# The opening of a linear-recurrence and feed-forward kernel: VectorE's queue in the order of the source, and half of the first stacking issued by ScalarE

## The chip, the core and the metric

The kernel runs on one core of a Trainium2 chip. The core has TensorE (PE: matrix products into PSUM; PEld is its loading of weights), VectorE (DVE), ScalarE (ACT), GpSimd (POOL) and SyncE (SP), each with its own queue of instructions that it runs in order, and 16 DMA engines that SP and ACT hand transfers to. The metric is device time in microseconds (us), the median of several runs; one more execution was recorded by the profiler, and the lines in this document are from it.

## The reference

For 4 batches, 8 heads, 768 tokens and head size 48, with a complex decay `a` per token and channel that is scaled to a magnitude of at most 0.999:

```python
mag = np.sqrt(a_re * a_re + a_im * a_im)
scale = np.minimum(mag, 0.999) / (mag + 1e-06)
a_re_n, a_im_n = (a_re * scale, a_im * scale)
for t in range(S):
    new_re = ar * S_re - ai * S_im
    new_im = ar * S_im + ai * S_re
    kv = np.einsum('bhd,bhe->bhde', k[:, :, t], v[:, :, t])
    S_re, S_im = (new_re + kv, new_im)
    y[:, :, t] = np.einsum('bhd,bhde->bhe', q[:, :, t], S_re)
```

Then `x`, the 3072 x 384 matrix of the `y`, goes through `(x @ w_a) * (x @ w_b) @ w_out` with `w_a`, `w_b` of 384 x 1536 and `w_out` of 1536 x 384. All in float32.

## The kernel before

The work is cut into 12 units: 2 pairs of batches times 6 chunks of 128 tokens. For each unit

- `scale(u)` works out the factor that limits the decay (ScalarE: squares, logarithms, exponentials; VectorE: the steps between, L178 to L192). In unit 0 it runs on two halves.
- `prep(u)` multiplies the decays up along the chunk (VectorE: `pr` and `z` at L226 and L232, the block products `pb` and `b_t` at L261 and L267, L288 and L293), takes magnitude and inverse (ScalarE L296, L303, L304 between VectorE's L293, L302, L317 and L319) and multiplies `q` and `k` by the result (`qk`, L308 and L323).
- `stack(u)` copies `qk` by ten small DMAs (eight heads, two of them in two pieces) into `stk`, with real and imaginary part of a head one below the other.
- `attn(u)` is the chunk's attention: scores on TensorE (L378), times a causal mask on VectorE (`am`, L381), outputs (L418), `x` split into a high and a low part (`xh`, `xl`; L422, L430, L433), and the carried state.
- The feed-forward: for each of 12 blocks `f` of 128 columns `gemm1` (L485, 18 products), the product of both halves on ScalarE and VectorE (`h_t`, `hh`, `hl`; L493 to L496), and two blocks later `gemm2` (L503, 6 products).

The weights come as float64 bits and are converted on the core, once, while unit 0 runs: `split_weights()` makes float32 from the bits with three VectorE instructions (L133, L135, L137, into one of three buffers `o_sb`), ScalarE rounds it to the high part (L141), TensorE forms the remainder (L146, L147), and ScalarE writes that as the low part (L148). There are 36 such conversions, three for each of the 12 blocks; `w26` is the third part of block 6. The first 21 (blocks 0 to 6) use `gemm1`'s three PSUM buffers `ab`, the others the buffers `pm` of the attention.

The order of the instructions on each engine is not the source's. A scheduler with its own model of costs puts every ready instruction in by priority (earlier in the source is more urgent, and `tc.high_priority` moves masks, `h_t` and casts further up). The order that comes out is fixed at build time. The source gives, ahead of the loop over the units: `scale(0)`, `prep(0)`, `stack(0)`, the conversions of blocks 0 to 5, then `attn(0)` with steps of `prep(1)`; in the loop of the first unit a block's conversions and a part of `prep(1)` stand ahead of each `gemm1`. `prep(u)` also runs `scale(u + 1)`. A unit's attention is interleaved with the feed-forward of the unit before.

Of the kernel before, what the change touches and what calls it, by code (L numbers as in the profile page):

```python
# [8 lines left out]
F32 = mybir.dt.float32  # L9
# [57 lines left out]
def tile_kernel(ctx: ExitStack, tc: tile.TileContext, a_d, qk_d, v_d, w_d, qn_d, kn_d, vn_d, an_d, out_d):  # L67
# [59 lines left out]
    def split_weights():  # L127
        for f in range(NF):
            for m, (c0, n) in enumerate(WPART):
                raw = raws[f, m]  # L130
                t = moe.tile([128, n], F32, name="o_sb", bufs=O_BUFS)
                tu = t.bitcast(U32)
                vec.tensor_scalar(out=tu, in0=raw[:, :, 1], scalar1=3, scalar2=0x3FFFFFFF,  # L133
                                  op0=ALU.logical_shift_left, op1=ALU.bitwise_and)
                vec.scalar_tensor_tensor(out=tu, in0=raw[:, :, 0], scalar=29, in1=tu,  # L135
                                         op0=ALU.logical_shift_right, op1=ALU.bitwise_or)
                vec.scalar_tensor_tensor(out=tu, in0=raw[:, :, 1], scalar=0xC0000000, in1=tu,  # L137
                                         op0=ALU.bitwise_and, op1=ALU.bitwise_or)
# [7 lines left out]
                pe.matmul(out=lp[:, 0:n], lhsT=ident, rhs=t, start=True, stop=False)  # L146
                pe.matmul(out=lp[:, 0:n], lhsT=r(nident), rhs=r(hi), start=False, stop=True)  # L147
                act.copy(out=r(lo), in_=lp[:, 0:n])  # L148
            yield


    bnext = {}
# [10 lines left out]
    halves = (slice(0, W // 2), slice(W // 2, W))  # L163
    z_first = zpool.tile([128, 3, W], F32, name="z")

    def scale(u, a_t, tmp):

        sc = zpool.tile([128, W], F32, name="sc")
        for n, hs in enumerate(halves if u == 0 else (slice(0, W),)):
            n = n and NU
            t = tmp[:, 0:2, hs]
            m, x, s0 = t[:, 0], t[:, 1], sc[:, hs]
            act.activation(out=t, in_=a_t[:, :, hs], func=AF.Square, accum_out=sums[:, u + n:u + n + 1])
            vec.scalar_tensor_tensor(out=m, in0=m, scalar=-EPS * EPS, in1=x, op0=ALU.add, op1=ALU.add)  # L178
            act.activation(out=s0, in_=m, func=AF.Ln, bias=b_sq)
            act.activation(out=s0, in_=s0, func=AF.Exp, scale=0.5)  # L180
            act.activation(out=s0, in_=s0, func=AF.Ln, bias=b_eps)
            act.activation(out=s0, in_=s0, func=AF.Exp, scale=-1.0)
            act.activation(out=x, in_=s0, func=AF.Square)
            yield 900
            vec.tensor_tensor(out=m, in0=m, in1=x, op=ALU.mult)
            act.activation(out=x, in_=s0, func=AF.Identity, scale=-EPS, bias=b_one)
            yield 900
            vec.scalar_tensor_tensor(out=m, in0=m, scalar=-0.5, in1=x, op0=ALU.mult, op1=ALU.add)
            yield 900
            vec.scalar_tensor_tensor(out=s0, in0=m, scalar=0.5, in1=s0, op0=ALU.add, op1=ALU.mult)  # L190
            yield 900
            vec.scalar_tensor_tensor(out=s0, in0=s0, scalar=0.999, in1=x, op0=ALU.mult, op1=ALU.min)  # L192
            yield 900
        sc_tiles[u] = sc

    def rescaled(c):
        return c % 2 == 1 and c + 1 < NCH

    def prep(u):
# [94 lines left out]
                              in0=view(pz[:], 0, PAIRS), in1=view(pz[:], W, PAIRS), op=ALU.add)  # L294
            yield 870
        act.activation(out=a_t, in_=z[:, 0:2], func=AF.Square)  # L296
        if rescaled(c):
# [7 lines left out]
        qk4 = qk[:, :, :, 0:2 * TOK].rearrange("p j s (x t) -> p j s x t", x=2)  # L305

        def times_p(k, x0, x1):
            vec.tensor_tensor(  # L308
                out=qk4[:, :, k, x0:x1], in0=qk4[:, :, 1, x0:x1],
                in1=z[:, k].rearrange("p (j t) -> p j t", j=NJ).unsqueeze(2).broadcast_to([128, NJ, x1 - x0, TOK]),  # L310
                op=ALU.mult)
# [25 lines left out]
    def stack(u):  # L337
        n = RUN if rescaled(u % NCH) else 2 * TOK
        for h in range(H):
            r0 = h * D  # L340
            while r0 < (h + 1) * D:
                j, p = divmod(r0, 128)
                m = min((h + 1) * D - r0, 128 - p)
                d0 = 2 * (r0 - h * D)
                sync.dma_start(out=stk[d0:d0 + 2 * m, h, 0:n], in_=qk[p:p + m, j, :, 0:n])
                r0 += m


    v_tiles = {}

    def load_v(u):
        for i in range(2):
# [11 lines left out]
    def attn(u, xh, xl):  # L364
# [8 lines left out]
        def scores(i, hg):  # L373
            qs, ks = cols(i)
            sp = ps_m.tile([128, 4, 128], F32, name="pm")
            for h4 in range(4):
                h = hg * 4 + h4
                pe.matmul(out=sp[:, h4], lhsT=stk[:, h, ks], rhs=stk[:, h, qs], start=True, stop=True)  # L378
            am = kvp.tile([128, 512], F32, name="am", bufs=2).rearrange("p (h t) -> p h t", h=4)
            with tc.high_priority(offset=ATTN_FIRST):  # L380
                vec.tensor_tensor(out=am, in0=sp, in1=mask[:].unsqueeze(1).broadcast_to([128, 4, 128]),  # L381
                                  op=ALU.mult)
            ams[i, hg] = am

        def transposes(i, hg):
# [260 lines left out]
    for w in range(NU):  # L646
        last = w + 1 == NU
        x_nxt = None if last else new_x()
        at = None if last else attn(w + 1, *x_nxt)
        if not last:  # L650
            load_v(w + 1)
        os_ = [ps_o.tile([128, 512], F32, name=f"o{t}") for t in range(2)]
        slots = [0, 2 * (STACK_AT[min(w, 4)] + 1 - max(ATTN_AT[min(w, 4)], 0 if w else P1_AT + 1))]
        left = [pieces(w + 1)]

        def slot():
            if at is None or f < ATTN_AT[min(w, 4)] or (w == 0 and f <= P1_AT) or not slots[1]:
                return
            n = -(-left[0] // slots[1])
            slots[1] -= 1  # L660
            for _ in range(n):
                next(at, None)
                left[0] -= 1

        for f in range(NF):
            if w == 0:
                next(ws, None)
                drain(p1, P1_F)
                if f == P1_AT:
                    drain(p1)  # L670
# [88 lines left out]
```

## Time and profile before

| | before |
|---|---|
| median of 3 runs | 700.21 us (699.59 to 700.63) |
| the profiled execution | 700.52 us, span 698.8 us |
| TensorE busy | 654.6 us (94%) |
| VectorE busy | 550.4 us (79%) |
| ScalarE busy | 311.4 us (45%) |

In the profile's lines a group is given as line, engine, operation, output<-input, shapes; in a timeline the first number is the start in us from the begin of the span, the second the duration in us, and the bracket at the end tells how long the engine had been idle and who ended that. `x2` means two instructions in a row. PEclk is TensorE's granted clock, 1.00 for full. SPq is SP handing out a DMA. A matmul in float32 that is not in the fast format shows as two records.

### The profile page before, as it was taken

The page shows a single profiled execution, that of the slowest core. Times are in us where ns is not written, and L with a number is a line of the kernel's source. Part 1 is how long each engine was busy: PE and PEld are TensorE (multiplying, and loading weights), DVE is VectorE, ACT ScalarE, POOL GpSimd, SP SyncE. Part 2 cuts the span into 40 slices and gives each one's busy share as a digit, 9 for nine tenths or more (in the row PEclk, how much of TensorE's full clock was granted, in tenths as well). Part 3 has the DMA queues.
Part 4 walks back from the last instruction along what each step waited for, and adds up shares of the span by engine and source line. Part 5 has one row for each costly group of instructions (what it writes and reads, how often), then busy time and mean ns, then how long its engine had stood idle before and what let it go on. Part 6 is the DMA issues. An engine that isn't in the chain of part 4 may idle for free.

```text
span 698.8 us, 14287 instructions
## 1 busy us (share of the span) xinstructions
PE 654.6 (94%) x5842; PEld 610.4 (87%) x5842; DVE 550.4 (79%) x1259; ACT 311.4 (45%) x622; POOL 5.6 (1%) x11
## 2 busy tenths in 40 slices
PE   3547999999999999999999999999999999999996
PEld 1224788799899999999999999999999999999996
DVE  6998899998888989989899798999989863233221
ACT  6357656634535446255363564534542332231221
POOL 3000000000000000000000000000000000000000
PEclk9567999999999999999999999999999999999999
DMA  8963300611414205124151340511510500300000
GB/s 312 403 262 93 120 1 0 180 58 58 130 38 130 81 21 157 58 88 132 32 161 45 93 143 2 166 69 47 135 55 2 162 27 17 106 23 2 24 1 27
DMA packets 30231, 63.93 MB, mean 91 GB/s; under 512 B 3664, under 2 KB 7248, under 8 KB 30160
## 3 DMA queue, kind: packets, MB, share of 16 engines
q1 hardware_dynamic: 26704, 58.23, 26.6%
q10 hardware_dynamic: 3456, 4.72, 1.9%
q8 instruction: 48, 0.79, 0.4%
q14 instruction: 23, 0.19, 0.1%
HBM read 39.32 MB, written 4.72 MB: 63 GB/s over the span
## 4 chain that ended last, share of the span: by engine, by line
PE 64%; DVE 26%; DMA 4%; ACT 3%; issue 2%; SPq 1%; DVEq 0%; ACTq 0%
PE ab L485 31%; PE o L503 15%; PE xp L418 6%; PE pm L378 4%; PE pm L441 4%; DVE a_t L288 2%; DMA w<-in_dram 2%; DVE pr L226 2%; DVE qk L308 2%; DVE h_t L494 2%; PE pm L389 2%; DVE hl L496 2%; DMA stk<-qk 1%; DVE am L381 1%; DVE z L232 1%
## 5 line engine op out<-in xcount | busy, mean ns | idle before, releaser
L485 PE MATMUL ab<-xh,w 128*128 128x256 f32 x1728 | 338.7, 285 | 0.0
L485 PEld LDWEIGHTS ab<-xh,w 128*128 128x128 f32 x1728 | 276.6, 189 | 1.9 <-issue 1.4
L485 PE MATMUL ab<-xl,w 128*128 128x256 f32 x864 | 244.6, 283 | 0.0
L485 PEld LDWEIGHTS ab<-xl,w 128*128 128x128 f32 x864 | 162.9, 189 | 0.5 <-ACT xl L433 0.2
L503 PE MATMUL o<-w,hh 128*128 128x384 f32 x576 | 152.4, 345 | 0.0
L493 ACT COPY h_t<-ab 128x256 f32<-128x256 f32 x144 | 53.3, 370 | 184.5 <-PE ab L485 184.1
L494 DVE TENSOR_TENSOR h_t<-ab,h_t 128x256 f32<-128x256 f32 x144 | 60.6, 421 | 70.5 <-ACT h_t L493 69.8
L503 PEld LDWEIGHTS o<-w,hh 128*128 128x128 f32 x576 | 96.8, 188 | 3.7 <-issue 2.8
L503 PE MATMUL o<-w,hl 128*128 128x384 f32 x288 | 97.6, 340 | 0.0
L495 ACT CAST hh<-h_t 128x256 fp32r<-128x256 f32 x144 | 58.0, 403 | 72.6 <-DVE h_t L494 71.4
L496 DVE TENSOR_TENSOR hl<-h_t,hh 128x256 fp32r<-128x256 f32 x144 | 60.6, 421 | 15.6 <-ACT hh L495 15.5
L378 PE MATMUL pm<-stk 128*128 128x128 f32 x384 | 55.3, 282 | 2.6 <-DMA stk<-qk 1.8
L146 PE MATMUL ab<-o_sb,ident 128*128 128x384 f32 x42 | 29.3, 797 | 29.9 <-DVE o_sb L137 29.9
L378 PEld LDWEIGHTS pm<-stk 128*128 128x128 f32 x384 | 49.6, 193 | 7.6 <-issue 4.2
L503 PEld LDWEIGHTS o<-w,hl 128*128 128x128 f32 x288 | 54.0, 188 | 0.1
L226 DVE TENSOR_TENSOR pr<-z 128x384 f32<-128x384 f32 (+1 forms) x91 | 47.2, 525 | 4.3 <-ACT z L212 2.5
L288 DVE TENSOR_TENSOR a_t<-z,b_t 128x768 f32<-128x768 f32 x48 | 45.1, 953 | 0.0
L146 PEld LDWEIGHTS ab<-o_sb,ident 128*128 128x128 f32 x42 | 10.2, 288 | 39.5 <-DVE o_sb L137 29.2
L418 PE MATMUL xp<-am,v_t 128*32 128x128 f32 x768 | 42.5, 277 | 2.1 <-DVE am L381 1.8
L308 DVE TENSOR_TENSOR qk<-qk,z 128x1536 f32<-128x1536 f32 (+1 forms) x26 | 42.3, 1628 | 0.1
L381 DVE TENSOR_TENSOR am<-pm,mask 128x512 f32<-128x512 f32 x48 | 32.8, 686 | 6.7 <-PE pm L378 6.6
L441 PEld LDWEIGHTS pm<-v_t,kt 128*96 128x96 f32 x320 | 32.2, 164 | 1.8 <-issue 1.4
(106 smaller groups left out, 758.7 us busy)
## 6 DMA issues: line engine op xcount, KB each, us to landing
w<-in_dram SPq DMA_DIRECT2D x36, 384.0 KB, 8.1
qk<-in_dram SPq DMA_DIRECT2D x12, 768.0 KB, 4.8
stk<-qk SPq DMA_DIRECT2D x48, 192.0 KB, 3.4
a_t<-in_dram SPq DMA_DIRECT2D x11, 768.0 KB, 4.4
v_t<-in_dram SPq DMA_DIRECT2D x24, 256.0 KB, 2.7
stk<-qk SPq DMA_DIRECT2D x24, 192.8 KB, 3.4
out_dram<-o_sb ACTq DMA_DIRECT2D x24, 192.0 KB, 1.9
stk<-qk SPq DMA_DIRECT2D x16, 128.0 KB, 3.1
```

Of the source, the lines that this page charges most:

```text
L226: vec.tensor_tensor(out=pr[:, :, :, o:o + n], in0=view(zz, W + at_(i) + 2 * o, [[W, 2], [-W, 2], [2, n]]), in1=tok(slice(1, 3), i - 1, o, ...
L288: vec.tensor_tensor(out=pz[:, s].rearrange("p (j b e) -> p j b e", j=SUB // 2, e=2), in0=zb[:, 1 + s], in1=view(bb, (1 + k - s) * NB, [[0, ...
L308: vec.tensor_tensor(out=qk4[:, :, k, x0:x1], in0=qk4[:, :, 1, x0:x1], in1=z[:, k].rearrange("p (j t) -> p j t", j=NJ).unsqueeze(2).broadca ...
L378: pe.matmul(out=sp[:, h4], lhsT=stk[:, h, ks], rhs=stk[:, h, qs], start=True, stop=True)
L418: pe.matmul(out=xp[qd * 32:(qd + 1) * 32, ti], lhsT=l, rhs=rr, start=st, stop=sp_, tile_position=(0, qd * 32), skip_group_check=True)
L441: pe.matmul(out=kp[0:KS, h4 * D:(h4 + 1) * D], lhsT=kts[i, hg][:, h4, :], rhs=v_t[:, o:o + D], start=True, stop=True)
L485: pe.matmul(out=ab[:, m * TOK:(m + 1) * TOK], lhsT=r(w_ab(f, part, m * NJ + i)), rhs=r(xt[:, i, :]), start=n == 0, stop=n == 8)
L493: act.copy(out=h_t, in_=ab[:, 0:TOK])
L494: vec.tensor_tensor(out=h_t, in0=ab[:, TOK:2 * TOK], in1=h_t, op=ALU.mult)
L495: act.copy(out=r(hh), in_=h_t)
L496: vec.tensor_tensor(out=r(hl), in0=h_t, in1=hh, op=ALU.subtract)
L503: pe.matmul(out=os_[tt][:, 0:DM], lhsT=r(ht[:, ts]), rhs=r(w_t[f, 2][:, part, :]), start=(f == 0 and n == 0), stop=(f == NF - 1 and n == 2))
```

## The change

Four things are changed, all in the first 150 us:

- VectorE's instructions from `scale(0)` to unit 0's fourth mask are issued under `tc.manual_schedule`: on VectorE they keep the order in which the source writes them. The conversions among them are put in by hand, in thirds (`split_weights` now yields ahead of each VectorE step), by the numbers `OPEN`.
- The two halves of `scale(0)` are generators of their own, and the multiplication of `qk` by the first power (`times_p(0, 0, 1)`) moves up by a few lines.
- Everything that VectorE gets after that, the rest of the conversions and of `prep(1)`, stands behind the last of the four masks (`tc.issue_after`); its order is the scheduler's again.
- In `stack(0)` the DMAs of the odd heads are handed out by ScalarE instead of SP.

```diff
+OPEN = (5, 1, 1, 2, 9, 3)
...
+                yield
                 vec.tensor_scalar(out=tu, in0=raw[:, :, 1], scalar1=3, scalar2=0x3FFFFFFF,
...
-            for k in range(2):
-                times_p(k, 0, 1)
+            times_p(1, 0, 1)
...
-                sync.dma_start(out=stk[d0:d0 + 2 * m, h, 0:n], in_=qk[p:p + m, j, :, 0:n])
+                eng = act if u == 0 and h % 2 else sync
+                eng.dma_start(out=stk[d0:d0 + 2 * m, h, 0:n], in_=qk[p:p + m, j, :, 0:n])
...
-    drain(scale(0, a_tiles[0], z_first))
-    drain(prep(0))
-    stack(0)
-    load_qk(1)
-    p1 = prep(1)
-    for _ in range(CONV_FIRST):
-        next(ws)
-    x_cur = new_x()
-    for _ in attn(0, *x_cur):
-        drain(p1, P1_A)
+    convert(1)
+    x_cur = new_x()
+    with tc.manual_schedule(engines={mybir.EngineType.DVE}):
...
+        next(g0)
+        next(g1)
+        convert(OPEN[0])
+        drain(g0)
+        convert(OPEN[1])
+        drain(g1)
+        p0 = prep(0)
+        for cost in p0:
+            if cost == 950:
+                convert(OPEN[2])
+            if cost == 1000:
+                convert(OPEN[3])
+        stack(0)
+        load_qk(1)
+        p1 = prep(1)
+        next(p1)
+        convert(OPEN[4])
+        next(p1)
+        convert(OPEN[5])
+        at = attn(0, *x_cur)
...
+    opening = latest[0].ins if hasattr(latest[0], "ins") else latest[0]
+    with tc.issue_after(opening):
+        convert(9 * CONV_FIRST - steps[0])
+        for _ in at:
+            drain(p1, P1_A)
```

Lines move a little: L133, L135, L137 become L135, L138, L141; the casts L141 and L148 become L145 and L152; L146 and L147 become L150 and L151; L178 to L192 become L180 to L194; L226 and L232 become L228 and L234; L308 becomes L302; L381 becomes L387; L485 becomes L491.

On VectorE, around the last step of the 21st conversion (of `w26`). Before (`o_sb_771` is its buffer, `w07` and `w17` are block 7):

```order
L133 TENSOR_SCALAR o_sb_771<-w26_168 128x384
L137 SCALAR_TENSOR_TENSOR o_sb_761<-w16_166,o_sb_761 128x384
L135 SCALAR_TENSOR_TENSOR o_sb_771<-w26_168,o_sb_771 128x384
L133 TENSOR_SCALAR o_sb_812<-w07_170 128x384
L137 SCALAR_TENSOR_TENSOR o_sb_771<-w26_168,o_sb_771 128x384
L135 SCALAR_TENSOR_TENSOR o_sb_812<-w07_170,o_sb_812 128x384
L137 SCALAR_TENSOR_TENSOR o_sb_812<-w07_170,o_sb_812 128x384
L133 TENSOR_SCALAR o_sb_822<-w17_172 128x384
L135 SCALAR_TENSOR_TENSOR o_sb_822<-w17_172,o_sb_822 128x384
L381 TENSOR_TENSOR am_519<-pm_514,mask_96 128x512
```

Now (`z_581` and `pr` are `prep(1)`, `a_t_144` and `sc_615` unit 2's `scale`):

```order
L135 TENSOR_SCALAR o_sb_773<-w26_168 128x384
L187 TENSOR_TENSOR a_t_144<-a_t_144 128x768
L228 TENSOR_TENSOR pr_642<-z_581 128x384
L138 SCALAR_TENSOR_TENSOR o_sb_773<-w26_168,o_sb_773 128x384
L234 TENSOR_TENSOR z_581<-pr_642 128x2x96
L190 SCALAR_TENSOR_TENSOR a_t_144<-a_t_144 128x768
L228 TENSOR_TENSOR pr_648<-z_581 128x384
L192 SCALAR_TENSOR_TENSOR sc_615<-a_t_144,sc_615 128x768
L234 TENSOR_TENSOR z_581<-pr_648 128x2x96
L194 SCALAR_TENSOR_TENSOR sc_615<-sc_615,a_t_144 128x768
L239 TENSOR_SCALAR z_581<-z_581 128x96
L141 SCALAR_TENSOR_TENSOR o_sb_773<-w26_168,o_sb_773 128x384
```

Before, that step stood ahead of unit 0's first mask; now it stands behind all four masks, seven steps of `prep(1)` and unit 2's `scale`.

On TensorE, at the first product of unit 0's feed-forward. Before, unit 0's attention (`xp`, `pm`) was in front of it and the 21st conversion 20 rows earlier:

```order
L418 MATMUL xp_587<-am_571,v_t_136 32x128 x6
L389 MATMUL pm_635<-ident_91,stk_108 128x96
L441 MATMUL pm_691<-v_t_134,kt_629 96x48 x4
L430 MATMUL xp_587<-xh_512,nident_115 128x384
L485 MATMUL ab_786<-xh_512,w00_336 128x256
```

Now the conversions of blocks 5 and 6 are in front of it:

```order
L150 MATMUL ab_572<-o_sb_566,ident_91 128x384
L151 MATMUL ab_572<-w25_570,nident_115 128x384
L150 MATMUL ab_759<-o_sb_576,ident_91 128x384
L151 MATMUL ab_759<-w06_757,nident_115 128x384
L150 MATMUL ab_769<-o_sb_763,ident_91 128x384
L151 MATMUL ab_769<-w16_767,nident_115 128x384
L150 MATMUL ab_779<-o_sb_773,ident_91 128x384
L151 MATMUL ab_779<-w26_777,nident_115 128x384
L491 MATMUL ab_790<-xh_201,w00_223 128x256
```

So the product that followed the attention now follows the last conversion of block 6.

On ScalarE, where the stacking is handed out (`a_t_118` and `sc_369` are unit 1's `scale`, `w01`, `w11` conversions of block 1):

```order
L179 ACTIVATE a_t_118,chk_104<-a_t_144 128x1536
L350 DMA stk_108<-qk_110 96x1x512 x2
L350 DMA stk_108<-qk_110 32x1x512
L350 DMA stk_108<-qk_110 64x1x512
L350 DMA stk_108<-qk_110 96x1x512
L181 ACTIVATE sc_369<-a_t_118,biases_99 128x768
L145 CAST w01_378<-o_sb_350 128x384
L182 ACTIVATE sc_369<-sc_369 128x768
L152 CAST w01_378<-ab_380 128x384
L183 ACTIVATE sc_369<-sc_369,biases_99 128x768
```

And on SP, whose queue had all weight loads and then ten stacking DMAs (the names in brackets are completion semaphores waited for; the first two stacking DMAs of ScalarE signal DMAHW4 and DMAHW6):

```order
L125 DMA w011_194<-in_3_dram 128x768 [waits DMAHW4_49]
L125 DMA w111_196<-in_3_dram 128x768 [waits DMAHW5_49]
L125 DMA w211_198<-in_3_dram 128x768 [waits DMAHW6_49]
L350 DMA stk_108<-qk_110 96x1x512 [waits DMAHW7_49,DVE_49]
L350 DMA stk_108<-qk_110 64x1x512 [waits DMAHW0_49]
L350 DMA stk_108<-qk_110 32x1x512 [waits DMAHW1_49]
```

Five stacking DMAs have moved from SP's queue into ScalarE's, between two steps of unit 1's `scale`; two of SP's last weight loads now wait for the first two of them.

More of the change, by code (lines that the diff above doesn't have):

```diff
@@ L148, in split_weights @@
                 act.copy(out=r(lo), in_=lp[:, 0:n])
-            yield
     bnext = {}
@@ L164, in tile_kernel @@
     z_first = zpool.tile([128, 3, W], F32, name="z")
[L166 to L193, printed above, removed]
@@ L296, in prep, with times_p @@
         act.activation(out=a_t, in_=z[:, 0:2], func=AF.Square)
+        qk4 = qk[:, :, :, 0:2 * TOK].rearrange("p j s (x t) -> p j s x t", x=2)
+        def times_p(k, x0, x1):
+            vec.tensor_tensor(
+                out=qk4[:, :, k, x0:x1], in0=qk4[:, :, 1, x0:x1],
+                in1=z[:, k].rearrange("p (j t) -> p j t", j=NJ).unsqueeze(2).broadcast_to([128, NJ, x1 - x0, TOK]),
+                op=ALU.mult)
+        if u == 0:
+            times_p(0, 0, 1)
+            yield 950
         if rescaled(c):
@@ L622, in tile_kernel, with convert @@
     ws = split_weights()
-    drain(scale(0, a_tiles[0], z_first))
-    drain(prep(0))
-    stack(0)
-    load_qk(1)
-    p1 = prep(1)
-    for _ in range(CONV_FIRST):
-        next(ws)
-    x_cur = new_x()
-    for _ in attn(0, *x_cur):
-        drain(p1, P1_A)
+    steps = [-1]
+    def convert(n):
+        for _ in range(n):
+            next(ws, None)
+            steps[0] += 1
+    convert(1)
+    x_cur = new_x()
+    with tc.manual_schedule(engines={mybir.EngineType.DVE}):
+        sc_first = zpool.tile([128, W], F32, name="sc")
+        g0, g1 = (scale(0, a_tiles[0], z_first, sc_first, n * NU, hs) for n, hs in enumerate(halves))
+        next(g0)
[18 more added lines that the diff above has]
+        at = attn(0, *x_cur)
+        for n in range(2):
+            next(at)
+        for n in range(3):
+            next(p1)
+        for n in range(4):
+            next(at)
+    opening = latest[0].ins if hasattr(latest[0], "ins") else latest[0]
[3 more added lines that the diff above has]
+            drain(p1, P1_A)
     pend = []
@@ L666, in tile_kernel @@
             if w == 0:
-                next(ws, None)
-                drain(p1, P1_F)
+                with tc.issue_after(opening):
+                    convert(9)
+                    drain(p1, P1_F)
+                    if f == P1_AT:
+                        drain(p1)
                 if f == P1_AT:
-                    drain(p1)
                     stack(1)
```

35 lines of the change are left out of this document (27 added, 8 removed).

## The prediction

> **What bounds the kernel now.** I read the busy times by stretch first, then TensorE's waits, then the rows of each engine in the first 150 us. Line numbers are those of the kernel before; "conversion" is one third of a weight block (L133, L135, L137 on VectorE, two casts on ScalarE, L146 and L147 on TensorE).
>
> ```profile
> core 0: us, PE busy (x) PEld busy (x) DVE busy (x) ACT busy (x) POOL busy (x), PEclk, DMA share, GB/s
> 0.00:77.00 77.00, 43.06 (x176) 23.70 (x176) 66.95 (x170) 42.53 (x80) 5.59 (x11) 0.76 0.72 259
> 77.00:160.00 83.00, 80.74 (x661) 72.25 (x661) 77.31 (x190) 47.77 (x99) 0.00 (x0) 1.00 0.20 60
> 160.00:300.00 140.00, 138.62 (x1358) 132.69 (x1357) 124.37 (x276) 65.44 (x122) 0.00 (x0) 1.00 0.28 84
> ```
> ```profile
> PE ab L146 <- DVE o_sb L137: 29.9, 13, 9.7
> ```
>
> From 77 us on TensorE is busy nearly without a gap, and stays so; before 77 us it waits, 29.9 us of it for VectorE's conversions. So what the opening costs is decided by when TensorE gets onto its dense work, and later stages give nothing back. The rows of TensorE (the first four from the timeline, the others from the chain of waits):
>
> ```profile
> 77.30 0.40 PE L485 MATMUL ab<-xh,w 128*128 128x256 f32 x2
> ...
> 82.79 0.81 PE L146 MATMUL pm<-o_sb,ident 128*128 128x384 f32 x2
> 83.14 0.63 PE L147 MATMUL pm<-w,nident 128*128 128x384 f32 x1
> 83.61 0.81 PE L146 MATMUL pm<-o_sb,ident 128*128 128x384 f32 x2
> ```
> ```profile
> 111.05 2.13 PE ab L485 x18
> 113.19 1.05 PE o L503 x6
> ...
> 130.99 0.49 PE pm L378 x2
> ...
> 149.56 0.43 PE ab L485 x3
> ```
>
> The first product of unit 0 starts at 77.30, the first of unit 1 at 149.56. In between lie 12 times 2.13 us of L485 (25.6), 12 times 1.05 us of L503 (12.6), 15 conversions of 0.82 us (start to start, 82.79 to 83.61; 12.3) and the attention of unit 1. Up to 130.99 (53.7 us) TensorE did all L485, ten L503 groups, the 15 conversions and 2.6 us of unit 0's attention: 51.0 us of work, so it ran 95% dense. The last 18.6 us are unit 1's attention with 2.3 us of L503 among it.
>
> **Where the change puts TensorE's start.** In the new order TensorE's first product of unit 0 stands directly behind L151 of the 21st conversion (block 6, third part). Before, that conversion was over at 63.4 us and the attention (76 to 77 us) was the last thing waited for. Now VectorE does far more ahead of it, so it becomes the gate. VectorE's rows:
>
> ```profile
> 8.42 0.56 DVE L135 SCALAR_TENSOR_TENSOR o_sb<-w,o_sb 128x384 uint32<-128x384 uint32 x1
> 9.02 0.56 DVE L137 SCALAR_TENSOR_TENSOR o_sb<-w,o_sb 128x384 uint32<-128x384 uint32 x1
> ...
> 11.56 0.55 DVE L185 TENSOR_TENSOR z<-z 128x384 f32<-128x384 f32 x1
> 12.03 0.55 DVE L137 SCALAR_TENSOR_TENSOR o_sb<-w,o_sb 128x384 uint32<-128x384 uint32 x1
> 12.80 0.56 DVE L188 SCALAR_TENSOR_TENSOR z<-z 128x384 f32<-128x384 f32 x1 [0.22 <-ACT z L186]
> ...
> 57.75 0.96 DVE L308 TENSOR_TENSOR qk<-qk,z 128x768 f32<-128x768 f32 x1
> 58.62 0.96 DVE L178 SCALAR_TENSOR_TENSOR a_t<-a_t 128x768 f32<-128x768 f32 x1
> ...
> 62.86 0.55 DVE L137 SCALAR_TENSOR_TENSOR o_sb<-w,o_sb 128x384 uint32<-128x384 uint32 x1
> ...
> 67.58 0.95 DVE L185 TENSOR_TENSOR a_t<-a_t 128x768 f32<-128x768 f32 x1
> ...
> 134.46 0.69 DVE L381 TENSOR_TENSOR am<-pm,mask 128x512 f32<-128x512 f32 x1 [0.36 <-PE pm L378]
> ```
> ```profile
> L226 DVE TENSOR_TENSOR pr<-z 128x384 f32<-128x384 f32 x14 | 7.8, 560 | 2.6 <-ACT z L212 2.3
> L381 DVE TENSOR_TENSOR am<-pm,mask 128x512 f32<-128x512 f32 x8 | 5.5, 686 | 1.4 <-PE pm L378 1.4
> L232 DVE TENSOR_TENSOR z<-pr 128x192 f32<-128x192 f32 x14 | 5.0, 357 | 0.2
> L188 DVE SCALAR_TENSOR_TENSOR a_t<-a_t 128x768 f32<-128x768 f32 x3 | 2.9, 953 | 0.0
> ```
>
> Neighbours overlap: 11.56 to 12.03 is 0.47 us for an instruction of 0.55, 57.75 to 58.62 is 0.87 for one of 0.96. So an independent instruction costs its duration less 0.09. One that reads its neighbour's result does not overlap: 8.42 to 9.02 is 0.60 where 0.47 would be due. I take 0.115 us more for each such pair, about the mean of the five that stand clear of other waits.
>
> - Base: L137 of the 21st conversion started at 62.86.
> - Added in front of it in VectorE's queue (counted in the two orders): the four masks L381 (4 x 0.60 = 2.4), nine 768-wide steps of `scale` (9 x 0.87 = 7.8), two L210 (1.7), seven pairs of L226 and L232 (7 x 0.73 = 5.1), less a step of a conversion (-0.3) and a short one (+0.1): 16.9 us.
> - Neighbours that depend: 65 pairs instead of 13, because conversions no longer stand between the steps of `prep(0)`. 52 x 0.115 = 6.0 us.
> - New waits. In the opening two naked waits for ScalarE's L186: 11.56 to 12.80 is 1.24, of which one conversion step filled 0.47 before: 2 x 0.77 = 1.5. For ScalarE's three steps between L293 and L317, which four conversion steps covered: 0.7 by the same bounds (0 to 2). In unit 2's `scale`: 0.5 (0 to 3). Waits of before that go: -0.9.
>
> The largest wait is unit 1's `scale`, whose five ScalarE steps now have the five stacking DMAs and casts ahead of or among them:
>
> ```profile
> 59.61 0.94 ACT L179 ACTIVATE sc<-a_t,biases 128x768 f32<-128x768 f32 x1 [0.21 <-DVE a_t L178]
> ...
> 63.37 0.48 ACT L148 CAST w<-ab 128x384 fp32r<-128x384 f32 x1 [0.71 <-PE ab L147]
> ```
> ```profile
> 58.74 6.78 SPq L345 DMA_DIRECT2D stk<-qk  x10
> ```
>
> Before, L178 to L185 took 8.96 us (58.62 to 67.58), the chain on ScalarE and casts that wait for TensorE (63.37, 0.71 us). VectorE has 5.1 us of work between these two in the new order (three conversions' worth of steps and L178 itself), so it stands at least 3.9 us; with five DMA issues of 0.68 us (6.78 / 10) ahead of the chain, of which 1.0 us is hidden, up to 6.3. I take 5.2. It can't wait below zero; if the casts no longer hold ScalarE, five steps of about 0.9 us (59.61) end after 5.2 us and the wait is near 0.
>
> New waits: 5.2 + 1.5 + 0.7 + 0.5 - 0.9 = 7.0 us. L137 of the 21st conversion then starts at 62.86 + 16.9 + 6.0 + 7.0 = 92.8, and from there the rest of L137 (0.55), the cast (0.5, as at 63.37) and L147 (83.14 to 83.61, 0.45) take 1.5 us: **94.3 us instead of 77.30**.
>
> **Unit 0's attention itself comes earlier, and that buys nothing.** 14 2/3 conversions of 1.21 us leave the front of the last L308: -17.7, +5.1 for 44 more dependent pairs, +1.3 net waits: it ends at about 47.4 instead of 58.7. The stacking: SP's row of ten DMAs becomes five on each queue, at best 3.4 us less. The masks follow only behind the wait of 5.2, at about 60 instead of 67. xh and xl are ready near 70, and TensorE may not use them until 94.
>
> **The sum.** From its start TensorE has, up to unit 1's first product, 25.6 + 10 x 1.05 + 12.3 + unit 1's attention (18.6 - 2.3 = 16.3 with its waits). In the new order three L485 groups stand among that attention, so its holes get filled; dense it would be 12.6. 61.0 dense, 64.7 as before; at 95% dense 64.2. Two L503 groups are left for later (2.1). 94.3 + 64.2 + 2.1 - 149.6 = +11.0 us. The profiled execution took 700.5 us (span 698.8), 0.3 above the median: **711**. After that both queues hold the same work, TensorE has no gaps to absorb a delay, and 0.2% (1.4 us) is what a measurement can tell from no change.
>
> [...]
>
> **Rivals.**
> 1. *VectorE's total, not TensorE's gate, sets the end (faster).* In the stretch before 135 us VectorE is the engine that TensorE meets. Its queue up to unit 1's first mask (134.46), added up as above, is 125.8 us, so 8.7 us are waits; the new queue to that mask is only 2.1 us longer (three h_t and hl pairs and some of `prep(2)` less, 46 more dependent pairs). If the new order has 5 us of waits, the end moves by 2.1 - 3.7 = -1.6: 698.9. It decides from 6.6 us of waits on downward. For it: VectorE is 87% busy before 77 us. Against: the 61 us that TensorE still has to do behind the gate.
> 2. *SP's half of the stacking arrives late (slower still).* In SP's new queue the last weight loads wait for ScalarE's stacking DMAs (they share completion semaphores), and SP's five stacking DMAs stand behind these loads. I have them landing some 11 us after the last L308, under the masks' 12.6. With loads as slow as the opening's (8.1 us to landing, below) they land at 16 us: +3.4, 714.5.
> [...]
> 4. *Hidden:* the gate opens at 77 as before, since the 17 us of added work were somehow run in idle time: 700.5. VectorE had about 10 us idle before 77, half of it ahead of the first data, so this needs a queue that isn't in order.
>
> ```profile
> w<-in_dram SPq DMA_DIRECT2D x36, 384.0 KB, 8.1
> ```
>
> **Chances and range.** My sum 66%, rival 1 10%, rival 2 12%, rival 3 8%, rival 4 4%. Slower by over 0.2%: 86% (the sum, 2, 3); within 0.2%: 6% (4 and the edge of 1); faster: 8% (1). The sum's own bounds: no new wait and dense TensorE gives 87.3 + 61.0 + 2.1 - 149.6 = +0.8; waits of 10 us and 67 us behind the gate give +17. Cutting the unlikely ends and keeping rivals 2 and 3: 703 to 718.
>
> **What would show it.** In the profile after: the last L308 of unit 0 (now L302) ends near 48; L187 of unit 1 about 10 us after L180, with VectorE idle some 5 us for ScalarE; the masks near 60; TensorE's first L491 at 94 (right if 90 to 98), with little on TensorE between 72 and 94; unit 1's first L491 near 159; from there the rows of before, some 11 us later. The forecast is wrong if that first L491 stands before 85, or if VectorE shows under 3 us of waits up to there.

## The result, and the profile after

The changed kernel takes 716.52 us (median of 4 runs, 716.39 to 716.87) where the kernel before takes 699.9 (4 runs, 698.8 to 700.63): 1.024 times as long, 95% interval 1.0222 to 1.0257. The forecast was 711 with a range of 703 to 718. The profiled execution spans 714.7 us against 698.8, so the traces compared here show 15.9 us of the difference. Line numbers below are those of the changed kernel: a conversion's three VectorE steps are L135, L138 and L141, TensorE's are L150 and L151, a mask is L387, a first-layer product L491.

First the busy times by stretch, in the columns of the prediction's first view:

```profile
core 0: us, PE busy (x) PEld busy (x) DVE busy (x) ACT busy (x) POOL busy (x), PEclk, DMA share, GB/s
0.00:77.00 77.00, 28.24 (x161) 17.18 (x162) 57.14 (x137) 32.45 (x60) 5.60 (x11) 0.96 0.74 263
77.00:160.00 83.00, 73.07 (x534) 58.79 (x532) 79.00 (x187) 51.47 (x105) 0.00 (x0) 0.92 0.17 48
160.00:300.00 140.00, 139.32 (x1327) 135.29 (x1320) 126.96 (x295) 66.63 (x128) 0.00 (x0) 1.00 0.29 87
...
0.00:99.74 99.74, 41.37 (x206) 23.61 (x206) 78.00 (x182) 48.57 (x91) 5.60 (x11) 0.92 0.59 208
```

Before 77 us VectorE did 57.14 us of work instead of 66.95, and TensorE 28.24 instead of 43.06. From 160 us on the rows are nearly those of before. The loss lies in the opening. TensorE's rows (timeline) show where it waits:

```profile
99.79 1.65 PE L150 MATMUL ab<-o_sb,ident 128*128 128x384 f32 x2 [5.46 <-DVE o_sb L141]
100.67 1.09 PE L151 MATMUL ab<-w,nident 128*128 128x384 f32 x1
101.56 0.41 PE L491 MATMUL ab<-xh,w 128*128 128x256 f32 x1
101.77 0.41 PE L491 MATMUL ab<-xl,w 128*128 128x256 f32 x1
...
110.19 0.28 PE L491 MATMUL ab<-xh,w 128*128 128x256 f32 x1
110.31 0.28 PE L491 MATMUL ab<-xl,w 128*128 128x256 f32 x1
...
165.96 0.36 PE L491 MATMUL ab<-xh,w 128*128 128x256 f32 x1
```

And unit 1's first product in the kernel before:

```profile
149.38 0.61 PE L485 MATMUL ab<-xh,w 128*128 128x256 f32 x3
```

The first product stands directly behind the L151 of the 21st conversion, as the order said, and that L150 waits 5.46 us for VectorE's L141. So the first product starts at 101.56 instead of 77.30 (+24.3), and unit 1's first comes 16.6 later (165.96 instead of 149.38; the 149.56 of the prediction is the same group in the chain of waits, which counts from the end of the piece before it). VectorE's rows show what made it late; in brackets is the idle time ahead of a row and what ended it:

```profile
11.83 0.56 DVE L190 SCALAR_TENSOR_TENSOR z<-z 128x384 f32<-128x384 f32 x1 [1.12 <-ACT z L188]
15.19 0.56 DVE L190 SCALAR_TENSOR_TENSOR z<-z 128x384 f32<-128x384 f32 x1 [0.68 <-ACT z L188]
39.18 0.96 DVE L315 TENSOR_TENSOR a_t<-a_t 128x768 f32<-128x768 f32 x1 [0.47 <-ACT a_t L298]
...
45.83 1.95 DVE L302 TENSOR_TENSOR qk<-qk,z 128x768 f32<-128x768 f32 x2
47.69 0.95 DVE L180 SCALAR_TENSOR_TENSOR a_t<-a_t 128x768 f32<-128x768 f32 x1
...
49.42 0.56 DVE L138 SCALAR_TENSOR_TENSOR o_sb<-w,o_sb 128x384 uint32<-128x384 uint32 x1
50.01 0.56 DVE L141 SCALAR_TENSOR_TENSOR o_sb<-w,o_sb 128x384 uint32<-128x384 uint32 x1
...
52.64 0.36 DVE L135 TENSOR_SCALAR o_sb<-w 128x384 uint32<-128x384 uint32 x1 [0.62 <-ACT w L145]
...
57.13 0.96 DVE L187 TENSOR_TENSOR a_t<-a_t 128x768 f32<-128x768 f32 x1 [3.54 <-ACT a_t L185]
...
62.77 0.69 DVE L387 TENSOR_TENSOR am<-pm,mask 128x512 f32<-128x512 f32 x1 [3.35 <-PE pm L384]
64.62 0.69 DVE L387 TENSOR_TENSOR am<-pm,mask 128x512 f32<-128x512 f32 x1 [1.16 <-PE pm L384]
...
70.29 1.02 DVE L138 SCALAR_TENSOR_TENSOR o_sb<-w,o_sb 128x384 uint32<-128x384 uint32 x2
...
93.23 0.96 DVE L187 TENSOR_TENSOR a_t<-a_t 128x768 f32<-128x768 f32 x1 [0.82 <-ACT a_t L185]
...
144.13 0.68 DVE L387 TENSOR_TENSOR am<-pm,mask 128x512 f32<-128x512 f32 x1
```

Up to the end of the 21st conversion's L141 VectorE was busy 78.00 of 99.74 us, so idle 21.74. For the kernel before the same cut gives 55.54 of 63.41, idle 7.87:

```profile
0.00:63.41 63.41, 31.71 (x60) 15.21 (x61) 55.54 (x153) 34.63 (x65) 5.59 (x11) 0.72 0.76 280
...
0.00:150.00 150.00, 113.80 (x755) 85.94 (x756) 134.53 (x334) 87.58 (x171) 5.59 (x11) 0.87 0.47 164
```

The 36.3 us by which that conversion is late are therefore 22.46 us of work and 13.87 us of new idle time. Two places have long waits: L187 of unit 1's scale with 3.54 us, and unit 0's first two masks with 3.35 + 1.16. In SP's and ScalarE's queues and in the times to landing (last column) the stacking looks like this:

```profile
24.89 27.33 SPq L125 DMA_DIRECT2D w<-in_dram  x16
52.33 4.50 SPq L350 DMA_DIRECT2D stk<-qk  x5
```
```profile
47.81 3.42 ACTq L350 DMA_DIRECT2D stk<-qk  x5
51.27 0.94 ACT L181 ACTIVATE sc<-a_t,biases 128x768 f32<-128x768 f32 x1 [4.56 <-DMA stk<-qk]
```
```profile
stk<-qk ACTq DMA_DIRECT2D x3, 192.0 KB, 3.3
stk<-qk SPq DMA_DIRECT2D x3, 192.0 KB, 5.9
```

ScalarE issues its five directly behind the last L302. SP's five start 4.6 us after that step's end (52.33 against 47.7), behind the last weight loads, and the three of 192 KB among them land in 5.9 us; in the kernel before, those of this size took 3.1.

### The profile page after: what moved, and what is told of

It reads as the page before. It is cut to its first block, busy times and chain, and to the rows that moved or that the text cites. A ratio compares the mean times of both kernels' runs of the same rounds, so it can differ in the third digit from the quotient of the medians.

```text
span 714.7 us, 14281 instructions
## 1 busy us (share of the span) xinstructions
PE 648.7 (91%) x5842; PEld 607.9 (85%) x5842; DVE 555.4 (78%) x1259; ACT 311.4 (44%) x622; POOL 5.6 (1%) x11
## 4 chain that ended last, share of the span: by engine, by line
PE 66%; DVE 24%; ACT 5%; DMA 2%; issue 1%; ACTq 0%; SPq 0%; DVEq 0%
PE ab L491 32%; PE o L509 16%; PE xp L424 6%; PE pm L384 5%; PE pm L447 4%; DVE a_t L290 2%; DVE pr L228 2%; PE pm L395 2%; DVE qk L302 2%; DMA stk<-qk 2%; DVE h_t L500 2%; DVE hl L502 2%; DVE z L234 1%; DVE pb L263 1%; DVE z L295 1%
## 5 line engine op out<-in xcount | busy, mean ns | idle before, releaser
L491 PE MATMUL ab<-xh,w 128*128 128x256 f32 x1728 | 339.6, 285 | 0.0
L491 PEld LDWEIGHTS ab<-xh,w 128*128 128x128 f32 x1728 | 277.7, 189 | 2.2 <-issue 1.7
L491 PE MATMUL ab<-xl,w 128*128 128x256 f32 x864 | 245.5, 284 | 0.0
L491 PEld LDWEIGHTS ab<-xl,w 128*128 128x128 f32 x864 | 163.5, 189 | 0.4
L150 PE MATMUL ab<-o_sb,ident 128*128 128x384 f32 x42 | 23.8, 670 | 50.5 <-DVE o_sb L141 50.5
L150 PEld LDWEIGHTS ab<-o_sb,ident 128*128 128x128 f32 x42 | 8.4, 243 | 56.6 <-DVE o_sb L141 45.3
L384 PE MATMUL pm<-stk 128*128 128x128 f32 x384 | 52.7, 281 | 1.7 <-DMA stk<-qk 1.7
L228 DVE TENSOR_TENSOR pr<-z 128x384 f32<-128x384 f32 (+1 forms) x91 | 47.2, 525 | 2.4 <-ACT z L214 0.4
L302 DVE TENSOR_TENSOR qk<-qk,z 128x1536 f32<-128x1536 f32 (+1 forms) x26 | 42.3, 1627 | 0.2
L387 DVE TENSOR_TENSOR am<-pm,mask 128x512 f32<-128x512 f32 x48 | 32.7, 684 | 7.5 <-PE pm L384 7.4
```

The source lines that it names most:

```text
L228: vec.tensor_tensor(out=pr[:, :, :, o:o + n], in0=view(zz, W + at_(i) + 2 * o, [[W, 2], [-W, 2], [2, n]]), in1=tok(slice(1, 3), i - 1, o, ...
L302: vec.tensor_tensor(out=qk4[:, :, k, x0:x1], in0=qk4[:, :, 1, x0:x1], in1=z[:, k].rearrange("p (j t) -> p j t", j=NJ).unsqueeze(2).broadca ...
L491: pe.matmul(out=ab[:, m * TOK:(m + 1) * TOK], lhsT=r(w_ab(f, part, m * NJ + i)), rhs=r(xt[:, i, :]), start=n == 0, stop=n == 8)
```

## The experiments

My theory was that TensorE's first product, held by the 21st conversion, sets the end, and that VectorE is late by its waits and by dependent neighbours. The rivals: VectorE's queue itself sets the end (TensorE's start is worth nothing by itself), and the stacking split is the cost. A ratio is to the kernel before on the same chip. The table has every kernel that ran, ordered by span; all but the ratio is from the profiled execution. For e1, e2 and e3 that execution was 1.4 to 2.2 us slower than the kernel's median, so these three spans are high by that much:

| kernel | first product | unit 1's first mask | VectorE busy, 0 to 150 us | span | ratio (95%) |
|---|---|---|---|---|---|
| e5: part 2 alone | 76.36 | 133.56 | 135.30 | 698.2 | 0.9997 (0.9988 to 1.0006) |
| before | 77.30 | 134.46 | 134.53 | 698.8 | 1 |
| e11: e5, thirds alternating | 78.02 | 131.15 | 134.35 | 698.9 | 1.0007 (0.9997 to 1.0018) |
| e9: all edits, order by hand | 80.68 | 138.15 | 132.91 | 702.2 | 1.0059 (1.0043 to 1.0076) |
| e8: e6, thirds alternating | 87.10 | 140.05 | 129.44 | 708.5 | 1.0143 (1.0124 to 1.0161) |
| e1: part 4 alone | 76.43 | 140.84 | 129.10 | 710.0 | 1.0136 (1.0115 to 1.0157) |
| e6: more thirds in the waits | 91.20 | 142.99 | 129.46 | 710.5 | 1.0177 (1.0161 to 1.0192) |
| e7: e6 and an earlier start | 81.14 | 136.58 | 129.59 | 711.7 | 1.0185 (1.0168 to 1.0203) |
| e4: earlier start | 81.18 | 130.08 | 127.66 | 712.8 | 1.0218 (1.0203 to 1.0234) |
| e3: conversions first | 91.10 | 147.91 | 126.10 | 712.8 | 1.0179 (1.0163 to 1.0194) |
| e10: without part 3 | 99.44 | 142.05 | 129.09 | 713.0 | 1.021 (1.0195 to 1.0226) |
| changed | 101.56 | 144.13 | 127.28 | 714.7 | 1.024 (1.0222 to 1.0257) |
| e2: without part 4 | 101.80 | 144.34 | 127.05 | 715.2 | 1.022 (1.0197 to 1.0243) |

### Which part of the change carries it

**e5**, parts 1, 3 and 4 undone:

```diff
-    with tc.manual_schedule(engines={mybir.EngineType.DVE}):
+    with ExitStack():
...
-    with tc.issue_after(opening):
-        convert(9 * CONV_FIRST - steps[0])
+    convert(9 * CONV_FIRST - steps[0])
...
-                eng = act if u == 0 and h % 2 else sync
+                eng = sync
```

> The changed kernel with parts 1, 3 and 4 undone: VectorE's queue left to the scheduler again, nothing tied behind the fourth mask, all stacking on SP; only part 2 stays (the opening's program order, two halves of scale(0), the earlier times_p). Theory (the order fixed by hand is the cause: its dependent neighbours and naked waits): VectorE's idle time up to the 21st conversion back near 8 us (21.7 in the changed kernel), first product at 76 to 79, time 699 to 702. Rival (the new program order costs by itself, whoever orders VectorE): 705 to 712.

Measured: 699.94 us, ratio 0.9997; VectorE's idle time up to the 21st conversion is 7.2 us. Part 2 costs nothing that can be told, so the loss lies in parts 1, 3 and 4 together.

**e10**, part 3 alone undone (both `issue_after` blocks taken out, the loop's too, as in the second edit above).

> The changed kernel with part 3 alone undone: nothing is tied behind the fourth mask. VectorE's order stays that fixed by hand, but the scheduler now places six conversion thirds between the masks. Theory (part 3 costs only what these thirds would have filled of the 4.5 us at the masks): 1 to 2.5 us less, 714 to 715.5. Rival (part 3 carries the loss): below 708. Rival (nothing): 716 to 717.

Measured: 714.78 us, 1.7 less than the changed kernel's median, as the theory had it; the two intervals just overlap. The mask waits fell from 4.51 to 2.60 us (2.32 + 0.28).

**e2**, part 4 alone undone (the third edit above).

> The changed kernel with part 4 undone: all ten stacking DMAs on SP. Theory (the masks' 4.5 us of waits come from SP's half standing behind weight loads that wait for ScalarE's DMAs, and ScalarE's 4.56 us of idle time in unit 1's scale from its own issues): SP starts the stacking at 48 instead of 52.3, L187 of unit 1's scale at 53 instead of 57.1, the first mask at 57 instead of 62.8, the 21st conversion's L141 at 93 to 95 instead of 99.2, first product at 95 to 97, time 710 to 712. Rival (ten issues on one queue cost as much as the hold-up did, or other waits take the place): 715 to 717. Rival (the split helps as it stands): 718 to 720.

Measured: 714.81 us; by the intervals this is not told from the changed kernel. VectorE's rows:

```profile
54.32 0.96 DVE L187 TENSOR_TENSOR a_t<-a_t 128x768 f32<-128x768 f32 x1 [1.36 <-ACT a_t L185]
59.73 0.69 DVE L387 TENSOR_TENSOR am<-pm,mask 128x512 f32<-128x512 f32 x1 [3.12 <-PE pm L384]
64.87 0.69 DVE L387 TENSOR_TENSOR am<-pm,mask 128x512 f32<-128x512 f32 x1 [4.45 <-PE pm L384]
```

SP's stacking did start at 47.88 and L187 came 2.8 us earlier, near the numbers expected. But the second mask stayed where it was (64.87; 64.62 in the changed kernel), and with it all that follows; the waits at the masks grew from 4.51 to 7.57 us. So the held-up queue was one cause of a wait that has a second one just behind it: the last stacking DMA had long landed (issued by 54.6, 3.2 us to landing), and TensorE's scores were late all the same. TensorE did them at about half its pace; first e2, then the kernel before:

```profile
61.47 3.36 PE L384 MATMUL pm<-stk 128*128 128x128 f32 x14
```
```profile
68.57 1.83 PE L378 MATMUL pm<-stk 128*128 128x128 f32 x14
```

That is 0.24 us a product instead of 0.13. In the kernel before the granted clock was 1.00 there; the changed kernel, at a granted clock of 0.50 between 60 and 62 us, shows the slow pace too (four in 1.06 us at 61.60). In e2 the column PEclk says 1.00 for this stretch, against the pace of its rows; that disagreement stays open. So undoing part 4 alone does not rid the changed kernel of its loss; what it would be worth with TensorE at full pace, e2 does not show.

With e10 and e2 neither part 3 nor part 4, undone alone, gives back more than about 2 us. What is left is part 1, the order fixed by hand. No kernel with part 1 and neither 3 nor 4 was run, so this is by exclusion; e9 below keeps the fixed order and wins most of the loss back by filling its waits, with part 4 undone.

**e1**, the kernel before with part 4 alone:

```diff
-                sync.dma_start(out=stk[d0:d0 + 2 * m, h, 0:n], in_=qk[p:p + m, j, :, 0:n])
+                eng = act if u == 0 and h % 2 else sync
+                eng.dma_start(out=stk[d0:d0 + 2 * m, h, 0:n], in_=qk[p:p + m, j, :, 0:n])
```

> The kernel before with part 4 of the change alone: the odd heads of unit 0's stacking issued by ScalarE. In this order of SP's queue no weight load waits for one of ScalarE's stacking DMAs. Theory (part 4 costs only where SP's queue is held by ScalarE's DMAs): ten issues on SP (6.78 us) become five on each, the masks of unit 0 come 1 to 3 us earlier than 67.0, TensorE's first product at 75 to 77 instead of 77.3, and the time is 698 to 700. Rival (two issuing engines cost by themselves: ScalarE's issues stand in the way of its casts): the masks at 68 or later, 701 to 704.

Measured: 710.32 us, ratio 1.0136. Both times that I gave were far off. TensorE's first product came 0.9 us earlier than before, as the theory had it, and the first mask at 66.77 instead of 66.98; yet the kernel lost 10 us. VectorE's and SP's rows, the times to landing, and TensorE's row at unit 1's attention:

```profile
66.77 0.69 DVE L382 TENSOR_TENSOR am<-pm,mask 128x512 f32<-128x512 f32 x1 [4.31 <-PE pm L379]
69.68 0.69 DVE L382 TENSOR_TENSOR am<-pm,mask 128x512 f32<-128x512 f32 x1 [0.77 <-PE pm L379]
71.87 0.69 DVE L382 TENSOR_TENSOR am<-pm,mask 128x512 f32<-128x512 f32 x1 [0.97 <-PE xp L419]
```
```profile
58.14 4.17 SPq L346 DMA_DIRECT2D stk<-qk  x5
...
134.08 6.02 SPq L346 DMA_DIRECT2D stk<-qk  x9
```
```profile
stk<-qk SPq DMA_DIRECT2D x3, 192.0 KB, 5.1
stk<-qk ACTq DMA_DIRECT2D x3, 192.0 KB, 5.4
```
```profile
137.52 2.32 PE L379 MATMUL pm<-stk 128*128 128x128 f32 x6 [4.47 <-DMA stk<-qk]
```

In this kernel's order the masks stand earlier in VectorE's queue, apparently because the scheduler takes ten DMAs on two queues to land sooner. Those of 192 KB land in 5.1 to 5.4 us instead of 3.1, and VectorE stands 6.05 us at three masks (1.00 in the kernel before). With that and its other changes of order, unit 1's stacking starts at 134.08 instead of 127.57. There the 10 us are lost: up to 125 us TensorE is as busy as before (47.77 of 48 us from 77 on; 47.66 before), then it waits 4.47 us for unit 1's stacking and does most of unit 1's attention at half pace (granted clock 0.50 from 137.5 to 153 us), so that unit 1's first product starts at 160.18, 10.8 us later than before. That a late VectorE costs time with TensorE starting early is the first strong evidence against my theory.

### What sets the end

**e3**, conversions ahead of unit 1's `prep`:

```diff
     with tc.issue_after(opening):
-        convert(9 * CONV_FIRST - steps[0])
+        with tc.high_priority(offset=4000):
+            convert(9 * (CONV_FIRST + 1) - steps[0])
...
-                    convert(9)
+                    convert(9 if f else 0)
```

> The changed kernel with the conversions up to the 21st given priority over unit 1's prep behind the fourth mask. VectorE's total up to unit 1's attention stays the same; only the seven pairs L228/L234 and unit 2's five scale steps move behind the 21st conversion. Theory: its L141 comes at 88 to 90 instead of 99.2, TensorE's first product at 90 to 92 instead of 101.6. If TensorE's start alone sets the end: 705 to 707. If VectorE's queue up to unit 1's first mask (144.1 now) sets it from here on: that mask stays at 143 to 146 and the time is 713 to 716. My own sum lies between: mask at 145, first product of unit 1 some 15.5 us behind it as in the kernel before, so 160.5 instead of 166.0 and 711.

Measured: 712.38 us. The first product came at 91.10, 10.5 us earlier, as expected; unit 1's first mask moved back to 147.91, later than the 143 to 146 expected, and only 4.1 us of the 10.5 reached the end.

**e4**, TensorE's first product behind 12 conversions instead of 21:

```diff
-CONV_ON_AB = 7
+CONV_ON_AB = 4
-CONV_FIRST = 6
+CONV_FIRST = 3
```

> The changed kernel with the first gemm1 group behind block 3's conversions (12 conversions) instead of block 6's (21); the later ones go among the products, into the other PSUM pool. VectorE's opening order is untouched. Theory (TensorE's first product standing behind the 21st conversion is what the change costs): first product near 80 instead of 101.6, VectorE reaches unit 1's first mask some 13 us earlier (30 conversions ahead of it instead of 36), first product of unit 1 at 148 to 151 instead of 166, time 698 to 704. Rival (the place in the queue doesn't matter, VectorE's total does, since all 36 conversions are needed anyway): 712 to 717.

Measured: 715.6 us. The first product at 81.18 and the mask at 130.08 were as expected; the time was not, it is the rival's. With an opened gate TensorE stands among the products instead:

```profile
100.00:125.00 25.00, 20.34 (x108) 15.43 (x107) 24.88 (x57) 12.85 (x27) 0.00 (x0) 1.00 0.11 36
```

VectorE is busy 24.88 of these 25 us and TensorE 20.34. The last conversion, which the last products of unit 0 need, starts on VectorE at 144.8 (138.2 in the changed kernel, 118.4 in the kernel before). Twenty microseconds of earlier start are worth 0.9, which by the intervals is not told from nothing. My theory falls: once the start is moved, what VectorE's queue still holds sets the end. In the changed kernel TensorE's start is the outer of the two limits, since e3 moved it and gained 4.1 with the mask even later; the inner one stands close behind. How close is not measured cleanly, because e3 and e4 moved VectorE's own steps as well.

**e6**, the waits filled: `OPEN = (5, 1, 1, 2, 18, 12)`, so that thirds which stood behind the masks stand in front.

> The changed kernel with more conversion thirds inside the opening: OPEN = (5, 1, 1, 2, 18, 12), so 18 stand between L180 and L187 of unit 1's scale and 12 ahead of the masks (9 and 3 in the changed kernel). No work is added; thirds that stood behind the masks fill the 3.54 us at L187 and the 4.5 us at the masks. Theory (VectorE's waits in the opening are lost for good, since both the 21st conversion and unit 1's prep stand behind them in one queue): 5 to 7 us of the waits go, the 21st conversion's L141 at 92 to 95 instead of 99.2, unit 1's first mask at 137 to 140 instead of 144.1, time 709 to 711.5. Rival (the added thirds wait for o_sb, whose casts stand in ScalarE's queue behind the same chain, so a wait is only renamed): 715 to 718.

Measured: 712.31 us, 4.2 less, by little short of the theory's range; unit 1's first mask came at 142.99, 1.1 us earlier and not the 4 to 7 expected. VectorE's rows in the place of the long waits:

```profile
52.74 0.36 DVE L135 TENSOR_SCALAR o_sb<-w 128x384 uint32<-128x384 uint32 x1 [0.56 <-ACT w L145]
56.05 0.36 DVE L135 TENSOR_SCALAR o_sb<-w 128x384 uint32<-128x384 uint32 x1 [1.76 <-ACT w L145]
58.50 0.36 DVE L135 TENSOR_SCALAR o_sb<-w 128x384 uint32<-128x384 uint32 x1 [0.90 <-ACT w L145]
...
72.03 0.69 DVE L387 TENSOR_TENSOR am<-pm,mask 128x512 f32<-128x512 f32 x1 [0.51 <-PE pm L384]
72.93 0.69 DVE L387 TENSOR_TENSOR am<-pm,mask 128x512 f32<-128x512 f32 x1 [0.20 <-PE pm L384]
```

Of 8.67 us between L180 and the last mask (0.62 + 3.54 + 3.35 + 1.16) 3.93 are left. Part of the rival is there too: the added thirds wait 1.76 and 0.90 us for ScalarE's cast L145.

**e7**, e6 with the start moved as in e4 (`CONV_ON_AB = 5`, `CONV_FIRST = 4`: 15 conversions).

> The edit of e6 and, as in e4, fewer conversions ahead of TensorE's first product (15: up to block 4). Theory of two limits that stand close together (TensorE's start, and VectorE's queue up to the last conversions and unit 1's attention): e4 opened the first alone and gained 1 to 2 us; with VectorE's waits filled as well the first product comes near 82 to 85 and the time is 705 to 709, less than e4 and e6 each. Rival (one limit, VectorE's queue: TensorE's start is worth nothing): the same as e6 within 1.5 us.

Measured: 713.4 us. First product 10 us earlier than in e6, and no gain (e6 had 712.31): the rival again.

**e8**, e6 with the thirds of two weight parts in turn (`split_one` holds the steps of one part):

```diff
+            pair = [split_one(*fm) for fm in order[k:k + 2]]
...
+            for _ in range(3):
+                for g in pair:
+                    yield
+                    next(g, None)
```

> The kernel of e6 with the conversions' thirds taken alternately from two weight parts, so that a third seldom reads the result of its neighbour. Same work, same number of thirds at each place. Up to the 21st conversion 52 pairs of dependent neighbours stand in VectorE's queue instead of 75. Theory (a dependent neighbour costs 0.115 us on VectorE): 23 x 0.115 = 2.6 us less VectorE time up to there; with e6 held by VectorE's queue the time falls from 712.3 to 709.5 to 711. Rival (dependent neighbours cost nothing): 711.8 to 712.8. Rival (two parts in hand need more o_sb buffers and wait for ScalarE's casts): 713 to 716.

Measured: 710.25 us, 2.1 less than e6, as the theory had it. The test is not clean: the two intervals touch, between 52 and 61 us VectorE waits 5.2 us ahead of the thirds that write o_sb, where e6 waits 3.2, and behind the masks the order differs a little. The price itself stands in the rows of the changed kernel: L138 to L141 of one part took 0.59 us (49.42 to 50.01), while two independent L138 took 1.02 together (70.29), 0.46 from start to start.

**e9**, all of it: e8, e3, e2, and two thirds more behind each L228/L234 step of `prep(0)` (`if cost == 440: convert(2)`).

> All of the edits together, the order still fixed by hand: e8, two thirds more behind each of the seven L228/L234 steps of prep(0), the 21 conversions ahead of unit 1's prep as in e3, all stacking on SP as in e2. Theory (the loss is made of VectorE's waits and dependent neighbours in the opening, and shrinks as these are filled): 45 dependent pairs up to the 21st conversion (63 in the changed kernel, 12 in the kernel before), the masks later than 70, unit 1's first mask at 138 to 141, time 704 to 708. Rival (some other property of the fixed order costs, such as TensorE's slow start): 710 to 714.

Measured: 704.58 us, inside the range, the mask at 138.15 as expected:

```profile
0.00:150.00 150.00, 104.22 (x689) 80.59 (x690) 132.91 (x319) 85.26 (x167) 5.59 (x11) 1.00 0.47 163
```

VectorE has done 132.91 us of work by 150 us, 1.6 less than before; the changed kernel was 7.3 behind (127.28). Three quarters of the loss are back (ratio 1.0059 of 1.024) with VectorE still ordered by hand. Which of its four edits brings how much is not shown beyond e2, e3 and e8.

**e11**, e5 with e8's turns, the control and the last candidate for a faster kernel.

> The kernel of e5 (VectorE ordered by the scheduler) with the alternate thirds of e8: the control for e8, and the one candidate left for a version faster than both kernels. The scheduler already keeps dependent neighbours apart: 15 such pairs up to the 21st conversion here, 12 in e5. Theory (alternating helps only where an order lacks independent neighbours): 699 to 701, no difference from the kernel before. Rival (alternating helps by itself, by freeing ScalarE's casts in pairs): 696 to 698.

Measured: 700.35 us, ratio 1.0007: no difference. None of these versions beats the kernel before.

## Why the prediction was right, and where not

- *The place of the gate: right.* The first product stands behind the L151 of the 21st conversion; the forecast 94.3 for it became 101.56, past the 98 that I had set as the end of "right".
- *Added work and dependent neighbours (16.9 + 6.0 = 22.9 us): right in sum.* VectorE's busy time up to there grew by 22.46; the two terms were not measured one by one.
- *New waits (7.0 us): the step that failed.* They are 13.9. The opening's two came to 1.80 (1.5 forecast), the one at L315 to 0.47 (0.7), L187 of unit 1 with the third ahead of it to 4.16 (5.2), L187 and L190 of unit 2 to 1.15 (0.5; L190's 0.33 is in the same view). What the sum lacked is 4.51 us at the masks, where I had none, and 1.1 us at three thirds behind them; those named come to 13.2, the rest are short gaps and the start, less the waits of before that went (0.98; 0.9 forecast). The masks' wait is rival 2's place, priced there at 3.4; e2 showed that its mechanism (SP's queue held by ScalarE's DMAs) is real and yet, taken away, gives back nothing that can be told, since TensorE's slow scores then held the second mask.
- *From L141 to the first product (1.5 us): 2.4*, TensorE being at half its clock there (below).
- *Unit 0's attention: right.* The last L302 ended at about 47.7 (47.4 forecast), and nothing came of it.
- *The way from the gate to unit 1: right.* 64.2 us were forecast, 64.4 measured (165.96 - 101.56), and two L503 groups were left over as forecast (60 records of the second layer in that stretch, 72 before). But the 2.1 us for them do not show at the end: from unit 1's first product on the changed kernel takes 548.7 us (714.7 - 165.96), the kernel before 549.4. So later stages did give something back, against the prediction. With the gate 7.3 later the sum would have given 718.3, 1.8 too much: the two errors are of opposite sign, and 711 lies as near as it does in part by that.
- *"What the opening costs is decided by when TensorE gets onto its dense work": only half right.* For the changed kernel the sum by the gate comes out roughly, since its gate is the later of two limits. It would have failed for e1, e4 and e7. What counts is how much TensorE has done, not when it began: up to 200 us the traces have 1225 matmul records in the kernel before, 1197 in e9, 1097 in e1, 1063 in e4 and 1037 in the changed kernel, in the order of their spans, and from 200 to 300 us TensorE is busy 99% or more in all five. That in turn hangs on VectorE. In the table the times follow how much VectorE has done by 150 us: above 134 us of work 698 to 699, 132.9 gives 702, around 129 give 708 to 713, 126 to 128 give 713 to 715; the first product at 76 to 81 is found with 698 as well as with 713. That is near to rival 1's statement, supported by this correlation and by e4 and e7; no run changes VectorE's queue and nothing else. Rival 1's price (698.9) was wrong because it let the waits fall, from 8.7 to 5 us. VectorE's idle time up to unit 1's first mask is 22.48 us (144.13 - 121.65) against 13.96 before (134.46 - 120.50), 8.5 more, and its work there 1.15 more (2.1 forecast); so that mask came 9.7 us later, not 1.6 earlier.
- *Rival 3* (dependent neighbours cost nothing) is refuted by 0.59 against 0.46 us in the rows named at e8 above, and the growth of 22.46 us fits with that: independent instructions start before their neighbour has ended, dependent ones do not. The Trainium skill, "VectorE: DVE Perf Modes", section "The DRAIN you can't avoid", says that the next operation does not start until the pipe is empty, but that one which is not held starts earlier; the independent rows here agree with the second (a start 0.46 us after that of an operation of 0.56 us). The section has no price for a dependent neighbour.

## What to carry to other kernels

An in-order queue written by hand pays for every wait and for every dependent neighbour that a mixed order had covered; before fixing such an order, count both up to the point where the next stage needs that engine, and put independent work into each. When two engines are busy nearly throughout, find the distance to the second limit before pricing the first: moving TensorE's start 20 us forward was worth 0.9, which is within the noise, since VectorE stood right behind. Spreading DMAs over two issuing queues is no gain where their landing, not their issue, is waited for.

## What the hardware showed that I had not expected

Two queues did not make the stacking's DMAs any faster here. On SP alone those of 192 KB land 3.1 us after their issue (kernel before); on two queues they take 3.3 and 5.9 (changed) or 5.1 and 5.4 (e1). The Trainium skill, "DMA: Bandwidth & Descriptors", section "Issuing engines are not separate DMA queues", says that DMAs started by several engines run on the same DMA engines and that only the time to issue them is saved. These rows agree: SP saves 2.6 us of issue in e1 (4.17 us instead of 6.78), and the transfers take 2.0 to 2.3 us longer.

TensorE came to its first products at half speed. The granted clock by stretch in the changed kernel, behind gaps of up to 5.46 us:

```profile
90.00:101.50 11.50, 5.16 (x9) 2.18 (x8) 10.35 (x26) 5.39 (x9) 0.00 (x0) 0.51 0.00 1
101.50:104.00 2.50, 2.50 (x13) 2.50 (x13) 2.50 (x11) 1.38 (x3) 0.00 (x0) 0.52 0.00 0
104.00:106.00 2.00, 2.00 (x14) 1.60 (x12) 1.86 (x11) 1.04 (x4) 0.00 (x0) 1.00 0.04 8
```

Products start 0.21 us apart at 101.56 and 0.12 at 110.19. The Trainium skill, "TensorE: Matmul & The Clock Gate", section "What's actually happening", has the clock at half after an idle window of about 3.4 us and full after as long a busy one. The rows agree: the gap was 5.46 us, and TensorE, dense from 99.79 us on, was at full pace from 103.91. A stage that has been starved starts slowly as well: the first eleven products took 2.35 us (101.56 to 103.91), 1.0 us more than at 0.12.
